# First batch of attention: where the probabilities are normalised and where the threshold is made

## The chip, the cores and the metric

One core of a Trainium2 chip runs the whole program. The metric is the device time of one execution in microseconds (us), as a median of several runs. The five engines appear in the profile as PE (TensorE matmul), PEld (TensorE's weight load, which overlaps PE), DVE (VectorE), ACT (ScalarE), POOL (GpSimd) and SP (SyncE, which issues the DMAs here). Each engine works through its own instruction list strictly in order.

## The reference

Attention with a threshold, then two feed-forward layers. Everything is float32.

```python
# q, k, v: (4, 8, 576, 64), tau = 0.02
scores = scale * q @ k.T                       # per batch and head, 576 x 576
thresh = max(scores, axis=-1) - tau
scores = where(scores >= thresh, scores, -1e9)
attn = exp(scores - max(scores)) ; attn = attn / (sum(attn) + 1e-9)
x = (attn @ v)  -> (2304, 512)
g = x @ w_gate ; x = (g * sigmoid(g) * (x @ w_val)) @ w_out      # 512 -> 1536 -> 512
h = max(x @ w_in, 0) ; out = (h * h) @ w_out2                    # 512 -> 2048 -> 512
```

## The kernel before

**Tiles.** Attention goes through 144 tiles of 128 query rows: 4 batches, 4 pairs of heads in each, 9 tiles in a pair. The first batch is tiles 0 to 35. The loop over `i` in `attention_moe` issues, for each turn, the steps of several tiles at different stages (`lag` is 2). The steps of one tile t are:

- QK: the scores on TensorE into one of two PSUM tiles `s` (t modulo 2).
- RED: the negated row maximum `nm` on VectorE (line 587).
- EXP: `e = exp(s + nm)` on ScalarE into one of three SBUF tiles `e` (t modulo 3), line 593, and right behind it the threshold `thr = -nm - tau`, a single column of 128 values, on ScalarE (line 595).
- MASK: one VectorE instruction multiplies `e` by `s >= thr` and sums each row (line 604). It is the last reader of `s`, so QK of tile t + 2 waits for it.
- RCP: the reciprocal `r` of the sum, one column, on VectorE (line 610).
- NORM: `e = e * r` over 128 x 576 values on GpSimd (line 615).
- TR: TensorE transposes the five 128-wide blocks of `e` into PSUM banks (line 635). It frees `e` for EXP of tile t + 3.
- PH, PL: copies of the transposed blocks from PSUM to SBUF, mostly on ScalarE in the first batch (the name `x` in the profile, line 48), a few on VectorE (line 50).
- AV: probabilities times values on TensorE (line 691 in the first batch, 694 later).

**Work beside it.** Throughout the first batch and the first half of the second one a loader turns the float64 weights into pairs of float32 pieces: each piece is a DMA (line 121), one ScalarE instruction (line 130), four VectorE instructions on 128 x 256 values (lines 132, 134, 138, 140), a ScalarE copy `w` (line 48) and a GpSimd subtraction `w` (line 56). For every coming pair of heads the queries and keys are split (`land` on ScalarE, `raw` on VectorE line 527 and on GpSimd line 56) and moved by DMA, a small block `qt` and the values `vs` are made on GpSimd (lines 52, 56). Once a batch's attention is done, its first feed-forward matmuls (line 219, input `xs_m`) fill TensorE between the tiles of the next batches. After attention TensorE runs the rest of the two layers.

**Order.** The instruction lists are fixed when the program is built. A scheduler sorts by the order of issue, shifted by offsets that the tables `early0` (first batch) and `early` (later) give each step; a step with a positive offset moves ahead of what was issued before it.

Of the kernel before, what the change touches and what calls it, by code (L numbers as in the profile page):

```python
# [14 lines left out]
ALU = mybir.AluOpType  # L15
# [4 lines left out]
B, H, S, D = 4, 8, 576, 64  # L20
# [42 lines left out]
def attention_moe(tc, qkv, qk0, tau, w1, w2, out, cfg):  # L63
    nc = tc.nc
# [8 lines left out]
    tau_n = cpool.tile([P, 1], F32, name="tau_n")  # L73
# [337 lines left out]
    for i in range(2):  # L411
        t = [ptp.tile([P, P], F32R, name=f"qt{i}{j}", tag=f"qt{i}{j}") for j in range(2)]
# [146 lines left out]
    st = [dict() for _ in range(NTILE + 8)]  # L559
# [30 lines left out]
    def EXP(t):  # L590
        e = es[t % len(es)]
        st[t]["e"] = e
        nc.scalar.activation(e[:, :S], st[t]["s"][:, :S], AF.Exp, bias=st[t]["nm"])  # L593
        if cfg["thr"] == "A":
            nc.scalar.activation(st[t]["thr"], st[t]["nm"], AF.Identity, scale=-1.0, bias=tau_n)  # L595
        else:
            e = nc.vector if cfg["thr"] == "D" else nc.gpsimd
            e.tensor_scalar(st[t]["thr"], st[t]["nm"], scalar1=-1.0, scalar2=tau_n, op0=ALU.mult, op1=ALU.add)

    def MASK(t):  # L600
        e = st[t]["e"]
# [10 lines left out]
    def NORM(t):  # L612
        e = st[t]["e"][:, :S]
        r = st[t]["r"]
        nc.gpsimd.tensor_scalar(e, e, scalar1=r, scalar2=1.0, op0=ALU.mult, op1=ALU.mult)  # L615

# [188 lines left out]
    for i in range(NTILE + lag + 1):  # L807
        mp1.age += 1
        fstate["i"] = i
        t = i - lag - 1  # L810
# [10 lines left out]
        if i < NTILE:  # L821
            at_(RED, i)
            at_(EXP, i)
# [7 lines left out]
        if 0 <= i - 1 < NTILE:  # L831
            at_(RCP, i - 1)
            at_(NORM, i - 1)
# [123 lines left out]
def pack(inputs):  # L957
# [15 lines left out]
    def cols(w, nf):  # L973
# [32 lines left out]
    "u1": ("P", "P"),  # L1006
    "u2": ("A", "D"),
    "qs": "A",
    "thr": "A",
    "wl": "PD",  # L1010
    "live": (3, 2),
    "fill": 6,
    "om": "A",
    "early0": {
        "AV": -2, "PS": 16, "NORM": 34, "EXP": 32, "LA": 20, "FP": -100, "PL": 30, "fill_group": -40,
        "RED": -12, "RCP": 4, "MASK": 4, "NEG": -60,
    },
    "three": 20,
# [29 lines left out]
```

## Time and profile before

| | us |
|---|---|
| median of 3 runs (1197.79 to 1198.41) | 1198.29 |
| the profiled execution | 1198.72 |
| span of its trace | 1196.9 |
| VectorE busy in the first batch, 11 to 113 us | 85.84 of 102.00 |
| TensorE busy in the same stretch | 94.18 of 102.00 |
| TensorE busy from 200 us on | 988.64 of 996.00 |

The span is what the trace covers; 1.8 us of the execution's own time lie around it. Busy times of TensorE are an upper reading, since its matmuls overlap and their ends are modelled. In the tables below, "idle before" is time in which an engine stood still ahead of an instruction, with the instruction that released it.

### The profile page before, as it was taken

To read this page: it belongs to the slowest core of one execution; us is meant where nothing else is said; L and a number is where in the kernel's file an instruction comes from. 1 tells how busy PE (TensorE), PEld (TensorE's weight loads), DVE (VectorE), ACT (ScalarE), POOL (GpSimd) and SP (SyncE) were. 2 spreads that over 40 slices of the span, in tenths; PEclk is the share of its full clock that TensorE was granted. 3 is DMA by queue.
4 is the path that set the end of the run, shared out by engine and by line. 5 is a ranking of instruction groups with operands and counts; after the bars stand their busy time and mean duration, and the time that the engine had idled before them with its cause. 6 is when DMAs were issued, how large, how long until landed. Compare 5 with 4: busy or idle time off the path is not lost.

```text
span 1196.9 us, 20191 instructions
## 1 busy us (share of the span) xinstructions
PE 1162.6 (97%) x7008; PEld 1074.8 (90%) x7008; DVE 868.2 (73%) x2143; ACT 652.1 (54%) x1622; POOL 293.8 (25%) x417
## 2 busy tenths in 40 slices
PE   5999998999999999999999999999999999999998
PEld 4555887999999999999999999999999899999997
DVE  6877997799989895789965954468449748754443
ACT  5777887888777774545432532145546425533221
POOL 4445875676776663000000000000000000000000
PEclk9999998999999999999999999999999999999999
DMA  5664452444334310332310300003002201100111
GB/s 177 151 182 127 127 134 66 109 116 110 94 97 106 93 36 1 108 104 80 98 36 7 108 29 1 1 18 104 21 1 80 62 1 54 36 1 1 53 54 53
DMA packets 40853, 84.79 MB, mean 71 GB/s; under 512 B 5936, under 2 KB 6960, under 8 KB 40752
## 3 DMA queue, kind: packets, MB, share of 16 engines
q1 hardware_dynamic: 40752, 83.52, 24.9%
q8 instruction: 55, 0.90, 0.3%
q14 instruction: 46, 0.38, 0.1%
HBM read 52.23 MB, written 4.72 MB: 48 GB/s over the span
## 4 chain that ended last, share of the span: by engine, by line
PE 79%; DVE 9%; DMA 3%; ACT 3%; issue 2%; POOL 2%; SPq 1%; POOLq 0%; DVEq 0%; ACTq 0%
PE mm L219 30%; PE mm L310 15%; PE mm L264 9%; PE s L575 5%; PE bank L635 5%; PE bank L219 4%; PE bank L264 4%; PE bank L694 4%; PE bank L691 3%; DMA wr<-in_w_dram 2%; DVE e L604 2%; DVE nm L587 1%; POOL e L615 1%; DMA raw<-in_qkv_dram 1%; DVE xs_k L56 1%
## 5 line engine op out<-in xcount | busy, mean ns | idle before, releaser
L219 PE MATMUL mm<-xs_k,w 128*128 128x384 f32 (+1 forms) x2400 | 413.2, 330 | 0.5 <-ACT x L48 0.5
L219 PEld LDWEIGHTS mm<-xs_k,w 128*128 128x128 f32 x2400 | 407.8, 188 | 2.5 <-ACT x L48 0.7
L310 PE MATMUL mm<-w,k_u 128*128 128x512 f32 x864 | 201.3, 391 | 0.3 <-DVE k_u L56 0.3
L310 PEld LDWEIGHTS mm<-w,k_u 128*128 128x128 f32 x864 | 161.5, 188 | 34.0 <-DVE k_u L56 1.0
L635 PE MATMUL bank<-ident,e 128*128 128x128 f32 x720 | 162.9, 278 | 6.4 <-POOL e L615 1.9
L219 PE MATMUL bank<-xs_m,w 128*128 128x288 f32 x720 | 137.1, 325 | 2.4 <-DVE xs_m L56 1.7
L615 POOL TENSOR_SCALAR e<-e,r 128x576 f32<-128x576 f32 x144 | 113.8, 791 | 83.6 <-DVE r L610 34.4
L604 DVE SCALAR_TENSOR_TENSOR e<-s,thr,e 128x577 f32<-128x577 f32 x144 | 117.0, 813 | 14.7 <-ACT thr L595 7.2
L48 ACT ACTIVATE k_u<-k_th 128x384 fp32r<-128x384 f32 (+1 forms) x148 | 76.3, 516 | 90.0 <-DVE k_th L294 47.0
L587 DVE TENSOR_REDUCE nm<-s 128x1 f32<-128x576 f32 x144 | 108.3, 753 | 17.7 <-PE s L575 16.6
L635 PEld LDWEIGHTS bank<-ident,e 128*128 128x128 f32 x720 | 95.2, 141 | 28.7 <-issue 15.9
L56 DVE TENSOR_TENSOR k_u<-k_th,k_u 128x384 fp32r<-128x384 f32 (+1 forms) x148 | 81.2, 549 | 47.8 <-ACT k_u L48 47.4
L219 PEld LDWEIGHTS bank<-xs_m,w 128*128 128x128 f32 x720 | 111.1, 189 | 5.1 <-DVE xs_m L56 3.4
L593 ACT ACTIVATE e<-s,nm 128x576 f32<-128x576 f32 x144 | 107.4, 746 | 14.3 <-PE bank L635 7.0
L655 ACT ACTIVATE pt<-bank 128x384 fp32r<-128x384 f32 (+1 forms) x216 | 92.1, 437 | 35.1 <-PE bank L635 28.9
L293 ACT ACTIVATE k_th<-mm 128x384 f32<-128x384 f32 x96 | 46.3, 483 | 111.0 <-PE mm L219 110.9
L264 PE MATMUL mm<-k_u,w 128*128 128x384 f32 (+1 forms) x624 | 106.1, 327 | 0.6 <-DVE k_u L56 0.4
L264 PEld LDWEIGHTS mm<-k_u,w 128*128 128x128 f32 x624 | 103.7, 188 | 1.0 <-DVE k_u L56 0.6
L694 PE MATMUL bank<-pt,vs 128*128 128x256 f32 (+1 forms) x480 | 93.5, 324 | 1.3 <-POOL pt L56 1.2
L575 PE MATMUL s<-kh,qs 128*128 128x288 f32 x256 | 78.1, 319 | 14.2 <-DVE qs L484 7.2
L294 DVE TENSOR_TENSOR k_th<-k_th 128x384 f32<-128x384 f32 x96 | 53.3, 555 | 52.4 <-ACT k_th L293 52.1
L48 ACT ACTIVATE w<-wf 128x256 fp32r<-128x256 f32 x116 | 46.8, 413 | 57.0 <-DVE wf L140 43.3
(90 smaller groups left out, 1697.0 us busy)
## 6 DMA issues: line engine op xcount, KB each, us to landing
wr<-in_w_dram SPq DMA_DIRECT2D x106, 256.0 KB, 3.0
raw<-in_qkv_dram SPq DMA_DIRECT2D x15, 896.0 KB, 4.7
kh<-land SPq DMA_DIRECT2D x60, 144.0 KB, 2.5
kl<-raw SPq DMA_DIRECT2D x60, 144.0 KB, 2.7
xF<-in_w_dram SPq DMA_DIRECT2D x30, 256.0 KB, 2.9
out_dram<-xF SPq DMA_DIRECT2D x18, 256.0 KB, 2.0
qs<-land SPq DMA_DIRECT2D x30, 144.0 KB, 2.4
qs<-raw SPq DMA_DIRECT2D x30, 144.0 KB, 2.6
```

The lines of the kernel that those rows point to most:

```text
L48: nc.scalar.activation(out, in_, AF.Copy)
L56: e.tensor_tensor(out, a, b, op=ALU.subtract)
L219: mm(pt[:, :n], w[:, a, col + c * P : col + (c + 1) * P], xs[:, b, c, :], start=(i == 0), stop=(i == len(TERMS) - 1),)
L264: mm(pt[:, :n], w[:, a, 2 * DM + m * P : 2 * DM + (m + 1) * P], u[:, b, :], start=(k == 0), stop=(k == last),)
L310: mm(pt, u[:, b, s * P : (s + 1) * P], w[:, a, DM : 2 * DM], start=(k == 0), stop=(k == last),)
L575: mm(sp[:, cols], l, r[:, cols], start=(n_ == 0), stop=(n_ == len(pairs) - 1),)
L587: nc.vector.tensor_reduce(nm, sv, axis=AX.X, op=ALU.max, negate=True)
L593: nc.scalar.activation(e[:, :S], st[t]["s"][:, :S], AF.Exp, bias=st[t]["nm"])
L604: nc.vector.scalar_tensor_tensor(e, st[t]["s"][:, : S + 1], st[t]["thr"], e, op0=ALU.is_ge, op1=ALU.mult, accum_out=sum_)
L615: nc.gpsimd.tensor_scalar(e, e, scalar1=r, scalar2=1.0, op0=ALU.mult, op1=ALU.mult)
L635: mm(dst[:, j], e[:, c0 : c0 + P], ident, is_transpose=True, start=(j == 0), stop=(j == len(cols) - 1),)
L694: mm(o[:, :n], hd["vs"][:, SLOT[k % 5], :], pt[:, k, lo : lo + n], start=(k == 0), stop=(k == 9))
```

## The change

In tiles 0 to 35 NORM goes from GpSimd to VectorE, with one multiplication in place of two, and the threshold goes from ScalarE to GpSimd. In the first batch's table the offset of NORM goes from 34 to 4, that of RCP. Later tiles keep both steps where they were.

```diff
@@ EXP
         nc.scalar.activation(e[:, :S], st[t]["s"][:, :S], AF.Exp, bias=st[t]["nm"])
-        if cfg["thr"] == "A":
+        if t >= cfg["normd"]:
             nc.scalar.activation(st[t]["thr"], st[t]["nm"], AF.Identity, scale=-1.0, bias=tau_n)
         else:
-            e = nc.vector if cfg["thr"] == "D" else nc.gpsimd
-            e.tensor_scalar(st[t]["thr"], st[t]["nm"], scalar1=-1.0, scalar2=tau_n, op0=ALU.mult, op1=ALU.add)
+            nc.gpsimd.tensor_scalar(st[t]["thr"], st[t]["nm"], scalar1=-1.0, scalar2=tau_n, op0=ALU.mult, op1=ALU.add)
@@ NORM
-        nc.gpsimd.tensor_scalar(e, e, scalar1=r, scalar2=1.0, op0=ALU.mult, op1=ALU.mult)
+        if t < cfg["normd"]:
+            nc.vector.tensor_scalar(e, e, scalar1=r, scalar2=None, op0=ALU.mult)
+        else:
+            nc.gpsimd.tensor_scalar(e, e, scalar1=r, scalar2=1.0, op0=ALU.mult, op1=ALU.mult)
@@ CFG
-    "thr": "A",
+    "normd": 36,
     "early0": {
-        "AV": -2, "PS": 16, "NORM": 34, "EXP": 32, "LA": 20, "FP": -100, "PL": 30, "fill_group": -40,
+        "AV": -2, "PS": 16, "NORM": 4, "EXP": 32, "LA": 20, "FP": -100, "PL": 30, "fill_group": -40,
```

The list of VectorE before, in the last pair of heads of the first batch, from MASK of tile 27 (sum_963) on: MASK, RCP and the loader's steps, and the reductions of tiles 29 and 30 (nm_999, nm_1030) between them.

```order
L604 SCALAR_TENSOR_TENSOR e_95,sum_963<-s_108,thr_932,e_95 128x577
L56 TENSOR_TENSOR xs_m_1340<-xF,xs_m_1340 128x288
L610 RECIPROCAL r_964<-sum_963 128x1
L604 SCALAR_TENSOR_TENSOR e_96,sum_994<-s_107,thr_970,e_96 128x577
L587 TENSOR_REDUCE nm_999<-s_108 128x1
L610 RECIPROCAL r_995<-sum_994 128x1
L587 TENSOR_REDUCE nm_1030<-s_107 128x1
```

The same place of VectorE's list now, where lines are numbered a little differently (603 is MASK, 609 RCP, 615 NORM):

```order
L603 SCALAR_TENSOR_TENSOR e_95,sum_963<-s_108,thr_932,e_95 128x577
L603 SCALAR_TENSOR_TENSOR e_96,sum_994<-s_107,thr_970,e_96 128x577
L609 RECIPROCAL r_964<-sum_963 128x1
L140 SCALAR_TENSOR_TENSOR xF<-xF 128x256
L615 TENSOR_SCALAR e_95<-e_95,r_964 128x576
L609 RECIPROCAL r_995<-sum_994 128x1
L132 TENSOR_SCALAR xF<-xF 128x256
L615 TENSOR_SCALAR e_96<-e_96,r_995 128x576
L587 TENSOR_REDUCE nm_999<-s_108 128x1
L134 TENSOR_SCALAR xF<-xF 128x256
L587 TENSOR_REDUCE nm_1030<-s_107 128x1
L138 SCALAR_TENSOR_TENSOR xF<-xF 128x256
```

Two tiles now go side by side: two MASKs, then the two NORMs among the loader's steps, then two reductions. The xs_m subtraction has left this place.

GpSimd's list before, at the preparation of the fifth pair of heads, with NORM of tiles 30 (r_1059) and 31 (r_1087):

```order
L615 TENSOR_SCALAR e_95<-e_95,r_1059 128x576
L52 TENSOR_SCALAR vs_1205<-raw_1020 128x5x64
L52 TENSOR_SCALAR vs_1275<-raw_1020 128x5x64
L56 TENSOR_TENSOR vs_1205<-raw_1020,vs_1205 128x5x64
L56 TENSOR_TENSOR vs_1275<-raw_1020,vs_1275 128x5x64
L56 TENSOR_TENSOR raw_1020<-raw_1020,land_1022 128x288 x2
L56 TENSOR_TENSOR w_2_145<-wf_78,w_2_145 128x256
L615 TENSOR_SCALAR e_96<-e_96,r_1087 128x576
```

The same place of GpSimd's list now (line 597 is the threshold; thr_1031 is that of tile 30, thr_1064 that of tile 31):

```order
L597 TENSOR_SCALAR thr_1031<-nm_1030,tau_n 128x1
L52 TENSOR_SCALAR vs_1275<-raw_1020 128x5x64
L56 TENSOR_TENSOR vs_1205<-raw_1020,vs_1205 128x5x64
L56 TENSOR_TENSOR vs_1275<-raw_1020,vs_1275 128x5x64
L56 TENSOR_TENSOR raw_1020<-raw_1020,land_1022 128x288 x2
L56 TENSOR_TENSOR w_2_145<-xF,w_2_145 128x256
L597 TENSOR_SCALAR thr_1064<-nm_1063,tau_n 128x1
```

The threshold of tile 31 stands where NORM of the same tile stood, behind the values, the keys and one weight piece.

At the end of the first batch VectorE's list now has the four xs_m subtractions of the first fill block almost together, behind the reduction of tile 38 (nm_1322):

```order
L587 TENSOR_REDUCE nm_1322<-s_108 128x1
L609 RECIPROCAL r_1316<-sum_1315 128x1
L56 TENSOR_TENSOR xs_m_1340<-xF,xs_m_1340 128x288 x3
L140 SCALAR_TENSOR_TENSOR wf_78<-xF,wf_78 128x256
L56 TENSOR_TENSOR xs_m_1340<-xF,xs_m_1340 128x288
```

Before, two of the four stood ahead of the first batch's end. From about tile 50 on the lists of VectorE and TensorE hold the same steps at the same tiles as before.

## Rows read from the trace of the kernel before

**Rows 1.** Busy time by stretch: stretch, length, then each engine's busy time (instructions).

```profile
core 0: us, PE busy (x) PEld busy (x) DVE busy (x) ACT busy (x) POOL busy (x), PEclk, DMA share, GB/s
11.00:113.00 102.00, 94.18 (x481) 58.40 (x482) 85.84 (x215) 76.70 (x196) 49.56 (x71) 1.00 0.55 145
113.00:140.00 27.00, 26.16 (x182) 22.98 (x181) 22.72 (x57) 22.07 (x62) 18.83 (x26) 1.00 0.45 128
140.00:170.00 30.00, 26.74 (x191) 24.53 (x190) 28.99 (x69) 25.18 (x68) 23.04 (x31) 1.00 0.49 132
170.00:200.00 30.00, 24.66 (x147) 21.73 (x147) 27.40 (x67) 22.98 (x60) 17.33 (x23) 0.89 0.34 95
200.00:1196.00 996.00, 988.64 (x6007) 945.17 (x6005) 699.77 (x1729) 501.81 (x1234) 179.60 (x252) 1.00 0.20 57
```

**Rows 2.** Waits, 11 to 113 us: who waited for whom, total, times, longest.

```profile
PEld s L575 <- DVE e L604: 8.4, 5, 4.4
...
DVE nm L587 <- PE s L575: 7.9, 14, 1.2
...
DVE e L604 <- ACT thr L595: 4.6, 5, 1.3
...
PEld bank L635 <- POOL e L615: 4.1, 7, 1.2
```

**Rows 3.** ScalarE's exponential and threshold, 11 to 113 us: groups, busy us, mean ns.

```profile
L593 ACT ACTIVATE e<-s,nm 128x576 f32<-128x576 f32 x38 | 28.2, 742 | 11.0 <-PE bank L635 7.0 <-DVE nm L587 1.4 <-POOL w L56 0.9
...
L595 ACT ACTIVATE thr<-nm,tau_n 128x1 f32<-128x1 f32 x37 | 10.6, 291 | 0.2 <-DVE nm L587 0.2
```

**Rows 4.** GpSimd's NORM and its smallest multiplication, 11 to 113 us, groups.

```profile
L615 POOL TENSOR_SCALAR e<-e,r 128x576 f32<-128x576 f32 x37 | 29.0, 787 | 35.2 <-DVE r L610 14.4 <-PE bank L635 4.7 <-ACT xF L48 4.2
...
L52 POOL TENSOR_SCALAR qt<-qs 128x64 fp32r<-128x64 f32 x9 | 2.5, 274 | 2.8 <-DMA qs<-raw 2.8
```

**Rows 5.** VectorE, 500 to 1190 us, where GpSimd is idle: groups by shape.

```profile
L56 DVE TENSOR_TENSOR k_u<-k_th,k_u 128x384 fp32r<-128x384 f32 x138 | 76.7, 556 | 47.6 <-ACT k_u L48 47.2
...
L138 DVE SCALAR_TENSOR_TENSOR wf<-wr,wf 128x256 int32<-128x256 int32 x100 | 41.8, 420 | 0.7
L56 DVE TENSOR_TENSOR w<-wf,w 128x256 fp32r<-128x256 f32 x101 | 41.7, 421 | 6.4 <-ACT w L48 5.9
...
L134 DVE TENSOR_SCALAR wf<-wf 128x256 int32<-128x256 int32 x100 | 28.6, 288 | 0.6
```

**Rows 6.** VectorE one after another: start, length, line; first near 27, then near 89 us.

```profile
27.21 0.29 DVE L132 TENSOR_SCALAR xF<-xF 128x256 f32<-128x256 f32 x1
27.42 0.16 DVE L610 RECIPROCAL r<-sum 128x1 f32<-128x1 f32 x1
...
89.00 0.76 DVE L587 TENSOR_REDUCE nm<-s 128x1 f32<-128x576 f32 x1 [0.94 <-PE s L575]
89.68 0.15 DVE L610 RECIPROCAL r<-sum 128x1 f32<-128x1 f32 x1
```

**Rows 7.** Busy time of VectorE's lines 132, 134, 138, 140, in that order.

```profile
11.00:113.00 102.00, 4.65 (x13) 1.00 0.55 145
...
11.00:113.00 102.00, 6.70 (x14) 1.00 0.55 145
...
11.00:113.00 102.00, 6.42 (x14) 1.00 0.55 145
...
11.00:113.00 102.00, 6.78 (x14) 1.00 0.55 145
```

**Rows 8.** VectorE's xs_m subtraction in the first batch, group of 11 to 113 us.

```profile
L56 DVE TENSOR_TENSOR xs_m<-xF,xs_m 128x288 fp32r<-128x288 f32 x3 | 1.7, 566 | 0.0
```

**Rows 9.** GpSimd in order of time near 98 us.

```profile
98.52 1.60 POOL L56 TENSOR_TENSOR raw<-raw,land 128x288 fp32r<-128x288 f32 x2
100.08 0.78 POOL L56 TENSOR_TENSOR w<-wf,w 128x256 fp32r<-128x256 f32 x1
100.84 0.74 POOL L615 TENSOR_SCALAR e<-e,r 128x576 f32<-128x576 f32 x1
```

## The prediction, made before the changed kernel ran

> **What bounds the kernel now.** I read the stretches first [rows 1]. From 200 us on TensorE is busy for 988.64 of 996 us, at full clock: nothing can be won there, and whatever the part before 200 us gains or loses arrives at the end unchanged. The change touches tiles 0 to 35, that is 11 to 113 us. In that stretch no engine is full: TensorE 94.18 of 102 us, VectorE 85.84, ScalarE 76.70, GpSimd 49.56. Next come the waits of that stretch [rows 2], which say why it still takes 102 us: TensorE and VectorE hold each other up. TensorE's QK stands 8.4 us for a MASK that has not freed its scores, its transposes 4.1 us for NORM; VectorE stands 7.9 us for scores and 4.6 us in MASK for the threshold, five times, up to 1.3 us. So the first batch is paced by a loop through four engines, and the engine with the least air after TensorE is VectorE, with 16.2 us. That is the engine that gets the work. Right behind, from 140 to 170 us, VectorE is busy 28.99 of 30 us: it can be run to 0.966, and it has no air to take over what the first batch leaves undone.
>
> **The change, part by part.**
>
> *The threshold leaves ScalarE.* 36 instructions of 0.291 us [rows 3]. ScalarE is not full, so the 10.5 us are worth only what waits for them: MASK need no longer wait for EXP and then for thr, but for the later of the two. Of the 4.6 us that MASK waited for thr the part behind EXP was about 5 x 0.29 = 1.5 us; the rest was EXP itself.
>
> *The threshold on GpSimd.* No row shows a one-column operation there. From above it is bounded by the 128 x 64 multiplication, 0.274 us [rows 4], from below by nothing; I take 0.2 us, nearer to the row, 36 x 0.2 = 7.2 us on an engine that gives up more. It starts with EXP from the same `nm` and has 0.742 us until EXP ends [rows 3], so it is hidden unless GpSimd is still at something else. If that cover goes, MASK waits, and behind MASK on VectorE's list stand RCP, NORM and the reductions, for which TensorE waits.
>
> *NORM leaves GpSimd.* 36 instructions of 0.787 us [rows 4]. TensorE's 4.1 us of waiting for it go. So does a queue: once, NORM starts only after 1.60 us of keys and 0.78 us of a weight piece [rows 9].
>
> *NORM on VectorE.* This is the price on which all hangs, and the trace of before has no VectorE multiplication of this size. The nearest rows: with GpSimd idle, the one-input, SBUF-to-SBUF step of line 134 takes 288 ns for 256 values, the two-input steps of the same width 420 and 421 ns, and 556 ns for 384 [rows 5]. Two-input work costs (556 - 421) / 128 = 1.055 ns a value; one-input work, at the same fixed part, half of that (421 - 0.5 x 1.055 x 256 = 286, the row says 288). NORM has one tensor input and a column of scalars. At the half rate it takes 288 + 320 x 0.527 = 457 ns, at the full rate 421 + 320 x 1.055 = 759 ns. Followed by the next instruction at once, it takes 0.08 us less of the engine's time: a 0.29 us step starts 0.21 us ahead of the next, a 0.76 us reduction 0.68 us ahead [rows 6]. So 36 x 0.38 = 13.7 us, or 36 x 0.68 = 24.5 us. I take 13.7: the operation is of line 134's kind, float32 in SBUF with one tensor input, and only the scalar's kind differs.
>
> The Trainium skill, "VectorE: DVE Perf Modes" (the perf-mode tier table), states the same split, 1227 ns against 2293 ns for 2048 float32 values, for tensor_scalar against tensor_tensor. An estimate from that page would be 0.46 us for NORM, which the trace's 0.457 us agrees with; the sum stays as it is.
>
> *What VectorE and GpSimd cost each other.* Lines 132 and 134 take 4.65 + 6.70 = 11.35 us for 27 instructions in the first batch [rows 7], against 27 x 0.288 = 7.8 alone [rows 5]: 3.6 us, 0.13 each, lost while GpSimd is busy 0.49 of the time. Lines 138 and 140 lose 6.42 + 6.78 - 28 x 0.420 = 1.4 us. NORM is 29.0 of GpSimd's 49.56 us [rows 1, 4]; with it gone 0.58 x 5.0 = 2.9 us of this loss go. GpSimd keeps 20.6 us and gets 7.2, 0.27 of the stretch, so a NORM on VectorE loses 0.13 x 0.27 / 0.49 = 0.07 us, 36 of them 2.6 us. Net: -0.3 us.
>
> A harder case: the Trainium skill, "SBUF — State Buffer" (SBUF: two separate sides), says that the port pair that VectorE's double-rate and two-input instructions share with GpSimd is an exclusive lock, held for a whole instruction while the other blocks. By it, a NORM that meets a GpSimd step of 0.78 us waits 0.39 us on average, in 0.27 of the cases, 3.8 us in all instead of 2.6: an estimate from that rule of 1197.1 us. Line 134's 0.13 us says less than the rule, which would make it 0.49 x 0.39 = 0.19.
>
> *What the scheduler moves along.* Two xs_m subtractions of 0.566 us [rows 8], 0.49 in a row, leave the first batch for the start of the second: -1.0 us here. There VectorE is busy 22.72 of 27 us [rows 1], so of the 1.0 us I count 0.4 as coming back.
>
> **The sum.** What VectorE has to do in the first batch: 85.84, minus 19 x 0.08 = 1.5 for the ends that show only because the two largest kinds of wait follow [rows 2, 6], plus 13.7, minus 0.3, minus 1.0, makes 96.7 us. With no wait at all the stretch would be 96.7 us, at the 0.966 of the second batch 100.1 us. I take 0.975, because two tiles now stand side by side in VectorE's list and each reduction has the partner's work ahead of it: 99.2 us, 2.8 less than 102. With the 0.4 us that come back, 2.4 us. TensorE allows it, at 94.18 us. The profiled execution took 1198.72 us (span 1196.9 and 1.8 around it), 0.4 above the median; the sum there is 1196.3, on the median's footing 1198.3 - 2.4 = **1195.9 us**. A difference under 0.2% (2.4 us) is about what a measurement of this kernel can't tell from none, and the forecast lies on that edge.
>
> **Rivals.**
>
> *VectorE becomes the bound (slower).* Place: VectorE's list in tiles 0 to 35. The stretch stays at 102 us only while VectorE's work stays under 102 x 0.975 = 99.5 us, that is while one NORM, port waits included, takes less than 0.45 + (99.5 - 96.7) / 36 = 0.53 us of the engine. At the full rate the work is 96.7 + 10.8 = 107.5 us, the stretch 110.3 us, the time 1207. At the half rate but with VectorE kept only 0.913 busy, as from 170 to 200 us (27.40 of 30) [rows 1], it is 105.9 us, and 1202.6. For it: 0.84 is all that VectorE reached in this stretch so far, and any loop through four engines loses something. Against it: two of that loop's links, thr behind EXP and NORM behind GpSimd's queue, are cut.
>
> *Hidden anyway (no change).* VectorE's air and TensorE's 4.1 us cancel, or the gain is given back from 113 to 200 us, where VectorE is at 0.97 and 0.91 and TensorE stands 3.3 and 5.3 us of 30 twice [rows 1], partly for the coming pairs' data, which a faster first batch does not bring. The same comes of a NORM that always sits out a whole GpSimd step (3.8 us of port waits, 1197.1). Time 1197 to 1200. For it: the lists hold the same steps from tile 50 on.
>
> *The threshold is stuck (slower).* In the new list thr of tile 31 stands behind the values, the keys and a weight piece. That is 1.60 + 0.78 = 2.4 us [rows 9] after the keys' input is there; VectorE has NORM, a reduction and loader steps to do meanwhile, some 2.5 us. If half of the keys' 1.60 us shows at each of 4 pairs, 3.2 us are lost, and the gain of 2.4 turns into 0.8 us of loss: 1199; if each of the 13 weight pieces delays a MASK by half its length too, another 5 us, 1204. It decides against the change from 2.4 us of such waits on.
>
> **Chances.** Forecast (1192.5 to 1198) 0.50, of which 0.37 lie below 1195.9 and 0.13 above; VectorE as the bound 0.20, of which 0.01 inside 0.2%; hidden anyway 0.20, of which 0.03 below, 0.14 inside and 0.03 above; the threshold stuck 0.10, of which 0.02 inside. Faster by over 0.2%: 0.37 + 0.03 = 0.40; same 0.13 + 0.01 + 0.14 + 0.02 = 0.30; slower 0.19 + 0.03 + 0.08 = 0.30. The range that keeps 8 in 10 begins at 1189.5: with no wait at all on VectorE the time is 1193, and TensorE, at 94.18 us, leaves room for a few us more. It ends at 1206, which takes in the half-rate case of the first rival and the stuck threshold and stops just short of the full rate.
>
> **What the next profile would show.** Right, if NORM on VectorE means 0.46 to 0.55 us; if the stretch from the first to the 37th reduction is 98 to 101 us; if VectorE is at least 0.96 busy in it; if MASK's waits for thr and the transposes' waits for NORM are near nothing; if from tile 50 on everything stands about 2.5 us earlier. Wrong, if NORM is 0.75 us, if QK waits for MASK by clearly more than 8.4 us, if MASK waits for thr on GpSimd, or if the second batch takes longer by what the first won.

## The result, and the profile of the changed kernel

The changed kernel takes 1213.78 us (median of 4 runs, 1211.85 to 1216.0) beside 1198.35 us of the kernel before: 1.0125 times as long, 95% interval 1.0102 to 1.0148. The forecast was 1195.9 us, with a range up to 1206 and 0.30 for slower. The profiled execution took 1216.0 us, its span is 1214.2.

The stretches of the changed kernel, in the columns of [rows 1]:

```profile
11.00:113.00 102.00, 87.51 (x434) 55.64 (x435) 87.37 (x218) 62.92 (x141) 31.13 (x65) 0.96 0.48 129
113.00:140.00 27.00, 24.95 (x128) 15.90 (x127) 20.28 (x52) 17.42 (x44) 8.97 (x14) 0.94 0.41 112
140.00:170.00 30.00, 27.64 (x202) 25.91 (x200) 28.80 (x71) 24.52 (x66) 23.96 (x33) 1.00 0.48 131
170.00:200.00 30.00, 24.42 (x163) 21.28 (x164) 29.03 (x68) 24.26 (x66) 20.90 (x28) 1.00 0.51 137
200.00:1196.00 996.00, 987.22 (x6013) 944.82 (x6012) 710.88 (x1757) 512.05 (x1262) 188.46 (x262) 1.00 0.20 56
```

In the first 102 us TensorE gets through 434 matmuls where it had 481 [rows 1], ScalarE through 141 instructions (of its 196 some 37 were thresholds). GpSimd fell from 49.56 to 31.13 us, as it should. But VectorE, with 36 more instructions of half a microsecond each in the batch, is busy 87.37 us, hardly more than the 85.84 before: it did not fill up, it waits. From 200 us on TensorE is as full as before. Nearly the whole loss is made by the first batch and its end.

To see how much of it is waiting, take the preparation of the seventh pair of heads on VectorE (line 527, the sixth of its kind; the first pair is prepared elsewhere) as a mark. It starts at 155.53 us before and at 171.41 after. Busy time up to that mark, first before, then after:

```profile
11.00:155.50 144.50, 134.34 (x763) 94.61 (x764) 123.17 (x308) 112.06 (x291) 79.64 (x111) 1.00 0.52 142
```

```profile
11.00:171.40 160.40, 140.52 (x761) 97.66 (x762) 137.84 (x343) 105.70 (x254) 64.80 (x112) 0.97 0.47 128
```

The same TensorE work, 761 and 763 matmuls, takes 15.9 us longer: 9.7 us of that is TensorE standing still (19.9 against 10.2 us), 6.2 us a longer busy time, to which a mean granted clock of 0.97 against 1.00 adds. The spans of these two traces differ by 17.3 us (1214.2 against 1196.9), so nearly all of the loss is there.

The waits of 11 to 113 us after the change, as in [rows 2]:

```profile
ACT x L48 <- PE bank L637: 17.4, 21, 2.5
PEld s L575 <- DVE e L603: 12.3, 12, 4.3
ACT xF L48 <- PE bank L693: 11.4, 11, 2.6
...
DVE e L603 <- ACT e L593: 6.5, 10, 1.4
DVE nm L587 <- PE s L575: 5.2, 6, 1.8
PEld bank L693 <- ACT x L48: 4.6, 11, 1.0
PEld bank L637 <- ACT x L48: 4.0, 5, 2.1
```

QK waits for MASK 12 times, 12.3 us, where it was 5 times, 8.4 us [rows 2]. The transposes' waits for NORM are small (1.0 us on the weight loads, 4.1 before), and MASK has no wait for the threshold in that stretch at all. What grew most are the rows with ScalarE in them. Its waits before, for the transposes and for AV, which [rows 2] does not hold:

```profile
ACT x L48 <- PE bank L635: 10.0, 17, 1.6
...
ACT xF L48 <- PE bank L691: 1.7, 4, 0.5
```

From 10.0 + 1.7 us they went to 17.4 + 11.4. Behind ScalarE, MASK stands for EXP, and AV and the transposes for ScalarE's copies.

One place shows how these hang together. Instructions of the changed kernel in order of time (start, length, engine):

```profile
90.20 2.91 PE L693 MATMUL bank<-x 128*64 128x320 f32 x10
...
90.47 0.52 DVE L615 TENSOR_SCALAR e<-e,r 128x576 f32<-128x576 f32 x1
90.90 0.16 DVE L609 RECIPROCAL r<-sum 128x1 f32<-128x1 f32 x1
...
91.93 0.76 DVE L587 TENSOR_REDUCE nm<-s 128x1 f32<-128x576 f32 x1
...
93.15 0.49 ACT L48 ACTIVATE xF<-bank 64x64 f32<-64x64 f32 x2 [2.58 <-PE bank L693]
...
94.20 0.77 ACT L48 ACTIVATE x<-bank 128x384 f32<-128x384 f32 x2
...
95.33 0.49 ACT L48 ACTIVATE x<-bank 128x384 f32<-128x384 f32 x1 [0.36 <-PE bank L637]
95.72 0.73 ACT L593 ACTIVATE e<-s,nm 128x576 f32<-128x576 f32 x1
95.87 2.37 PE L693 MATMUL bank<-x 128*64 128x256 f32 x10 [0.36 <-ACT x L48]
...
96.55 0.82 DVE L603 SCALAR_TENSOR_TENSOR e<-s,thr,e 128x577 f32<-128x577 f32 x1 [1.39 <-ACT e L593]
...
98.17 0.40 PE L575 MATMUL s<-kh,qs 128*128 128x288 f32 x1
```

TensorE does an AV as one block from 90.20 on. ScalarE has the copies of its output next in its list and stands 2.58 us for them (before, the longest such wait is 0.5 us). The row maximum that EXP needs is there at 92.69, but EXP stands behind those copies, a weight piece and the copies of two tiles, and starts at 95.72, 3.0 us late. MASK on VectorE waits 1.39 us for it, and the next QK comes at 98.17, behind the next whole AV. No engine is busy beyond its means here; each does, in order, what its list says next.

The added and moved instructions themselves (count; shortest, median and longest in ns; first and last start):

```profile
L615 DVE TENSOR_SCALAR e<-e,r x36: 500/515/1060, 14.6 to 128.3; 128x576 f32<-128x576 f32 x36
```

```profile
L597 POOL TENSOR_SCALAR thr<-nm,tau_n x36: 262/268/643, 12.0 to 121.7; 128x1 f32<-128x1 f32 x36
```

### The profile page after: what moved, and what is told of

It is laid out like the page before. It is cut to its first block, busy times and chain, and to the rows that moved or that the text cites. A ratio compares the mean times of both kernels' runs of the same rounds, so it can differ in the third digit from the quotient of the medians.

```text
span 1214.2 us, 20139 instructions
## 1 busy us (share of the span) xinstructions
PE 1168.4 (96%) x7008; PEld 1077.5 (89%) x7008; DVE 884.5 (73%) x2179; ACT 646.6 (53%) x1586; POOL 278.4 (23%) x417
## 4 chain that ended last, share of the span: by engine, by line
PE 80%; DVE 10%; ACT 3%; DMA 3%; issue 2%; POOL 1%; SPq 0%; POOLq 0%; DVEq 0%; ACTq 0%
PE mm L219 32%; PE mm L310 16%; PE mm L264 8%; PE s L575 5%; PE bank L637 5%; PE bank L219 4%; PE bank L264 4%; PE bank L693 3%; PE bank L696 3%; DVE e L603 2%; DVE nm L587 2%; DMA xF<-in_w_dram 1%; DMA wr<-in_w_dram 1%; DVE xs_m L56 1%; DVE pt L56 1%
## 5 line engine op out<-in xcount | busy, mean ns | idle before, releaser
L603 DVE SCALAR_TENSOR_TENSOR e<-s,thr,e 128x577 f32<-128x577 f32 x144 | 116.9, 814 | 17.4 <-ACT e L593 11.6
L617 POOL TENSOR_SCALAR e<-e,r 128x576 f32<-128x576 f32 x108 | 86.0, 796 | 56.3 <-DVE r L609 28.6
L323 DVE TENSOR_TENSOR xF<-xF,mm 128x512 f32<-128x512 f32 x54 | 37.0, 686 | 55.8 <-PE mm L310 55.8
```

The source lines that it names most:

```text
L603: nc.vector.scalar_tensor_tensor(e, st[t]["s"][:, : S + 1], st[t]["thr"], e, op0=ALU.is_ge, op1=ALU.mult, accum_out=sum_)
```

## The experiments

Times in the table are medians, the ratio is to the kernel before in runs on the same chip, with its 95% interval. Kernels have their own line numbers; where a row is shown, the text says what it is.

| run | NORM / threshold on | lists | us | ratio |
|---|---|---|---|---|
| norm_only | VectorE / ScalarE | scheduler | 1216.7 | 1.0147 (1.0132 to 1.0162) |
| thr_only | GpSimd / GpSimd | scheduler | 1205.7 | 1.0053 (1.0038 to 1.0068) |
| norm_pinned | VectorE / ScalarE | of before | 1201.8 | 1.0021 (1.0011 to 1.0030) |
| thr_pinned | GpSimd / GpSimd | of before | 1201.5 | 1.0019 (1.0003 to 1.0035) |
| both_pinned | VectorE / GpSimd | of before | 1203.2 | 1.0041 (1.0026 to 1.0056) |
| lists_of_after | GpSimd / ScalarE | of after | 1215.9 | 1.0140 (1.0125 to 1.0155) |
| col1_lists_before | VectorE, 1 column / GpSimd | of before | 1196.2 | 0.9980 (0.9965 to 0.9995) |
| col1_lists_after | VectorE, 1 column / GpSimd | of after | 1211.8 | 1.0104 (1.0081 to 1.0126) |
| after_pe | VectorE / GpSimd | TensorE's of before | 1219.3 | 1.0175 (1.0158 to 1.0191) |
| after_act | VectorE / GpSimd | ScalarE's of before | 1218.8 | 1.0166 (1.0147 to 1.0186) |
| after_dve | VectorE / GpSimd | VectorE's of before | 1219.0 | 1.0173 (1.0150 to 1.0196) |
| free_dve | VectorE / GpSimd | of before, but VectorE's | 1215.8 | 1.0139 (1.0117 to 1.0161) |
| before_pairs | GpSimd / ScalarE | scheduler, one rule | 1200.3 | 1.0010 (0.9999 to 1.0021) |
| control_av | GpSimd / ScalarE | scheduler, other offset | 1201.0 | 1.0016 (1.0004 to 1.0029) |
| after_alt | VectorE / GpSimd | scheduler, one rule | 1209.0 | 1.0086 (1.0070 to 1.0101) |
| before_alt | GpSimd / ScalarE | scheduler, one rule | 1217.6 | 1.0155 (1.0135 to 1.0176) |
| norm_later | VectorE / GpSimd | scheduler, other offset | 1214.0 | 1.0127 (1.0109 to 1.0145) |
| after_tr3 | VectorE / GpSimd | scheduler, one rule | 1223.7 | 1.0206 (1.0187 to 1.0226) |

**Each move alone.** The offset of NORM (34 or 4) does not change a single row of any list, with either engine, so it needed no run. The two moves:

```diff
+        nc.scalar.activation(st[t]["thr"], st[t]["nm"], AF.Identity, scale=-1.0, bias=tau_n)   # norm_only
-        if t < cfg["normd"]:
-            nc.vector.tensor_scalar(e, e, scalar1=r, scalar2=None, op0=ALU.mult)                # thr_only
+        nc.gpsimd.tensor_scalar(e, e, scalar1=r, scalar2=1.0, op0=ALU.mult, op1=ALU.mult)
```

> NORM of tiles 0 to 35 on VectorE, the threshold stays on ScalarE; the lists come out new, as in the changed kernel. Theory of the lists (the fixed order of TensorE, ScalarE and VectorE that came out with the change stalls the first batch, not the added work): 1203 to 1216 us, by how bad these lists are. Theory of the work (36 NORMs at about 0.5 us are simply added to the loop over tiles): 1211 to 1216 us. Theory of the threshold (GpSimd makes it too late): about 1198 us.

> The threshold of tiles 0 to 35 on GpSimd, NORM stays on GpSimd. Theory of the lists: 1197 to 1206 us, these lists stand nearer to those of before. Theory of the work: 1195 to 1199 us, ScalarE loses 10 us and VectorE gains none. Theory of the threshold: about 1214 us.

NORM alone makes the whole loss, so the threshold is not needed for it. The threshold alone loses too, 6.4 us (beside 1199.3), but nothing comes on top when both move. These two runs leave open whether NORM's time or the new lists cost it.

**The lists held.** Edges that fix only the order of issue, between neighbours on one engine, make a kernel keep a list that another one had:

```diff
+    for earlier, later in zip(order, order[1:]):      # one list for each engine
+        tc.add_manual_dep(later, earlier.name,
+            mybir.DependencyInfo(mybir.DependencyClass.NoSync, mybir.DependencyReason.DATA), reason="order")
```

> NORM of tiles 0 to 35 on VectorE, directly behind RCP, and otherwise every engine keeps the list of the kernel before, instruction by instruction. Theory of the lists: 1196 to 1201 us, since VectorE's gaps in the first batch take up the added work. Theory of the work: 1210 to 1216 us, as in the changed kernel. Theory of the threshold: about 1198 us.

> The engines of the kernel before (NORM on GpSimd, threshold on ScalarE behind the exponential), but TensorE, ScalarE, VectorE and SyncE keep the lists of the changed kernel. Theory of the lists: 1209 to 1216 us, the loss comes with the lists though no work was moved. Theory of the work: 1196 to 1200 us. Theory of the threshold: about 1198 us.

> The whole change (NORM on VectorE behind RCP, threshold on GpSimd), but every engine keeps the list of the kernel before for all the rest; only the place of the threshold in GpSimd's list is the scheduler's. If the lists are the whole loss: 1197 to 1203 us, near the run with NORM alone in the lists of before (1201.8). If threshold and NORM together cost something that neither does alone: 1208 us or more.

> The threshold of tiles 0 to 35 on GpSimd, and every engine keeps the list of the kernel before for all the rest. If a threshold on GpSimd beside the exponential is hidden: 1195 to 1200 us. If it is late behind GpSimd's other work, or slowed beside VectorE, and MASK waits for it: 1202 to 1208 us.

This decides between lists and work. The whole change in the lists of before loses 4.6 us; the work of before in the lists of the changed kernel loses 16.5 us (beside 1199.3 on the same chip), with not one instruction moved to another engine. The profile of that second kernel, 11 to 113 us (line numbers of before), has the waits of the changed kernel, not those of its own engines:

```profile
ACT x L48 <- PE bank L635: 16.6, 21, 2.3
DVE e L604 <- ACT thr L595: 14.8, 20, 1.6
...
ACT xF L48 <- PE bank L691: 10.4, 10, 2.5
...
PEld bank L691 <- ACT x L48: 5.1, 12, 1.2
PEld bank L635 <- ACT x L48: 4.0, 4, 2.4
```

And both_pinned, with VectorE's added work in the lists of before, hasn't (line numbers of the changed kernel):

```profile
PEld s L575 <- DVE e L603: 14.7, 14, 4.4
...
ACT x L48 <- PE bank L637: 6.6, 13, 1.8
PEld bank L637 <- ACT x L48: 3.3, 5, 1.0
...
ACT xF L48 <- PE bank L693: 2.2, 4, 0.7
DVE e L603 <- ACT e L593: 1.4, 2, 0.8
```

```profile
11.00:113.00 102.00, 91.41 (x459) 56.49 (x460) 95.34 (x241) 68.49 (x152) 37.52 (x69) 1.00 0.52 138
```

ScalarE is no longer stuck, VectorE is busy 0.935 of the stretch, and what QK waits for is MASK behind VectorE's own work. norm_pinned and both_pinned end 0.8 and 0.2 us above the ranges given for the lists, and far below the 1208 and 1210 us of their rivals. thr_pinned came out between its two expectations: a threshold on GpSimd is not a gain even in the old lists.

**NORM's time alone.** The two runs below keep every row of all five lists and cut only the width of NORM:

```diff
-            nc.vector.tensor_scalar(e, e, scalar1=r, scalar2=None, op0=ALU.mult)
+            nc.vector.tensor_scalar(e[:, :1], e[:, :1], scalar1=r, scalar2=None, op0=ALU.mult)
```

> The changed kernel with all lists kept as they are, but NORM of tiles 0 to 35 works on one column of 576 (so the first batch is hardly normalised). VectorE loses 36 times some 0.45 us, 16 us. If the lists by themselves stall the first batch: 1206 us or more, most of the loss stays. If the changed lists only put NORM's 0.5 us on the path, tile after tile: 1194 to 1200 us. Between the two, the loss divides.

> The changed kernel in the lists of before (1203.2 us with whole NORMs), NORM of tiles 0 to 35 on one column of 576 (so the first batch is hardly normalised). If the 4.6 us lost in these lists are NORM's time on VectorE: 1195 to 1199 us. If they come from the threshold on GpSimd or from elsewhere: 1201 to 1204 us.

With both_pinned and the changed kernel they make a square. In the lists of before NORM's time is worth 1203.2 - 1196.2 = 7.0 us; in the lists of after 1213.8 - 1211.8 = 2.0 us, no more than the runs of either scatter. The lists are worth 10.6 us with whole NORMs and 15.6 us without. A NORM of one column takes 0.21 us, a whole one in the mean 0.56 us in the lists of before and 0.59 in those of after, so the cut takes 12.5 and 13.8 us of VectorE's work away, less than the 16 expected. In col1_lists_after ScalarE sits out the same wait for the same AV, though NORM takes 0.2 us:

```profile
91.88 0.75 DVE L587 TENSOR_REDUCE nm<-s 128x1 f32<-128x576 f32 x1
93.70 0.49 ACT L48 ACTIVATE xF<-bank 64x64 f32<-64x64 f32 x2 [2.58 <-PE bank L693]
...
96.28 0.74 ACT L593 ACTIVATE e<-s,nm 128x576 f32<-128x576 f32 x1
```

**What in the lists.** First one engine's list at a time, with the edges above:

> The changed kernel with TensorE's list of before; the other lists come out of the scheduler under that. If the order of TensorE (probabilities times values in whole blocks ahead of the scores) is the loss: 1198 to 1204 us. If it is ScalarE's or VectorE's order, whose lists here stand about as far from before as from the changed kernel: 1208 to 1216 us.

> The changed kernel with ScalarE's list of before (less the thresholds); the other lists come out of the scheduler under that, TensorE's then much like that of before, VectorE's not. If ScalarE's or TensorE's order is the loss: 1198 to 1204 us. If VectorE's order is: 1208 to 1216 us.

> The changed kernel with VectorE's list of before (NORM directly behind RCP); the other lists come out of the scheduler under that and stand as far from before as the changed kernel's do. If VectorE's order (two MASKs, two NORMs and two reductions together) is the loss: 1198 to 1204 us. If TensorE's or ScalarE's order is: 1208 to 1216 us.

None of the three brings anything back; each is 5 us slower than the changed kernel and above both ranges of its expectation. Holding one list is thus no cure. It clears no engine's order either, since the lists that were left free moved again. Then rules and offsets:

```diff
+    chain_(tc, [x_ for k in range(36) for x_ in (reds[k + 1], masks[k])])                        # after_alt, before_alt
+    chain_(tc, [x_ for k in range(1, 36, 2) for x_ in (reds[k], reds[k + 1], masks[k], masks[k + 1])])  # before_pairs
+    for k in range(2, 35): chain_(tc, [qks[k + 3], trs[k][0]])                                    # after_tr3
-        "AV": -2, "PS": 16, "NORM": 34,
+        "AV": -6, "PS": 16, "NORM": 34,                                                           # control_av
-        "AV": -2, "PS": 16, "NORM": 4,
+        "AV": -2, "PS": 16, "NORM": -30,                                                          # norm_later
```

> The changed kernel with one rule more for VectorE's list of the first batch: reductions and MASKs alternate (RED of tile t + 1, MASK of tile t, RED of t + 2, MASK of t + 1), where the changed kernel has two reductions and then two MASKs; all else is the scheduler's. Theory of the pairs (the two score tiles are freed together, so TensorE and VectorE wait for each other): 1198 to 1206 us. Theory of the kept balance (the lists of before fit the durations on the chip by their tuned offsets, and any other set of lists loses, whatever its kind): 1208 to 1220 us.

> The kernel before (NORM on GpSimd, threshold on ScalarE) with one rule more for VectorE's list of the first batch: two reductions, then the two MASKs, as in the changed kernel; all else is the scheduler's. Theory of the pairs: 1208 to 1216 us. Theory of the kept balance: 1203 to 1212 us, some loss as with any other lists.

> The kernel before with the offset of AV in the first batch's table at -6 in place of -2: no work is added, removed or moved to another engine, but a quarter of TensorE's and a fifth of VectorE's rows of the first batch come in another order. Theory of the pairs: 1196 to 1202 us, since reductions and MASKs still mostly alternate. Theory of the kept balance: 1203 to 1212 us.

Two theories of mine fell here. Pairs of reductions and MASKs cost the kernel before nothing that can be told (1.0010). Nor does just any rearrangement cost much: the control lost 0.16%. What helped the changed kernel a little, alternation, is not good in itself, as before_alt shows below.

> The changed kernel with one number other: the offset of NORM in the first batch's table is -30 in place of 4, so that the scheduler puts NORM, and with it the transposes and their copies, later. In TensorE's list the transposes of tile t stand behind the scores of tile t + 3 for 31 of 32 tiles (19 of 32 in the changed kernel, 30 of 32 before). Theory of the distance (short distance makes TensorE and ScalarE, in order, wait for tile t's own chain before they go on with t + 2 and t + 3): 1199 to 1206 us. Rival (lists that the scheduler makes with NORM on VectorE are bad in VectorE's own order, between loader and loop): 1210 to 1220 us.

> The changed kernel with one rule for TensorE's list: the transposes of tile t stand behind the scores of tile t + 3 (all 32 tiles, 19 of 32 without the rule); ScalarE's copies come later by that for some tiles only. Theory of the distance: 1201 to 1209 us, not all of it, since the copies still stand behind the exponential of t + 1 for 10 of 32 tiles. Rival: 1210 to 1220 us.

> The kernel before (NORM on GpSimd, threshold on ScalarE) with the rule of the earlier run that VectorE's reductions and MASKs alternate in the first batch; by it the transposes of all 32 tiles stand behind the scores of t + 2 only. Theory of the distance: 1205 to 1212 us, like the changed kernel with the same rule (1209.0). Rival: 1197 to 1203 us, as in the other runs with NORM on GpSimd.

> The changed kernel with the lists of before on TensorE, ScalarE, GpSimd and SyncE; VectorE's list alone is the scheduler's. Distances as before. Theory of the distance: 1201 to 1206 us, near the run with all lists of before (1203.2). Rival (VectorE's own order): 1210 to 1220 us.

The theory of the distance fell as well: norm_later has the long distance and stays at 1214, after_tr3 has it and is the slowest of all. free_dve is the clearest of the four: four engines have the lists of before, and VectorE's, made by the scheduler, still loses 12.6 us against both_pinned. So a new order on VectorE alone is enough to lose the time. It is not the only way: after_dve, with VectorE's list of before, takes 1219.0 us, and before_alt loses with no work moved. norm_later and free_dve came out in the range of their rival, VectorE's own order, after_tr3 and before_alt above both of theirs. Up to 113 us free_dve has a wait that the kernel before does not have, ScalarE standing for weight pieces that come later in VectorE's list than ScalarE's list reckons with:

```profile
ACT w L48 <- DVE xF L140: 11.1, 4, 3.8
...
ACT w L48 <- DVE wf L140: 3.1, 1, 3.1
```

So the lists of before work as a set. One pattern goes through all the slow runs, those of 1209 us and more: what stands behind ScalarE waits in order. Up to 113 us either AV's weight loads wait 4.4 us or more for ScalarE's copies, or MASK waits 10.1 us or more for EXP (after_act, free_dve, after_pe, after_tr3). In the kernel before and in all runs up to 1206 us the first is 2.3 us at most and the second 9.3. That is read off the traces, the limits were picked with the times in hand, and 9.3 and 10.1 lie close together; no run changed either wait alone, so it is not shown as the cause.

## Why the prediction was wrong, by its own steps

**The step that failed** is "I take 0.975, because two tiles now stand side by side in VectorE's list and each reduction has the partner's work ahead of it". VectorE was busy 87.37 of 102 us, 0.857, and 0.850 from the first reduction to the 37th. The new lists were in front of me, and I read them on VectorE alone, as a gain. In their place the runs showed a loss: by the square above the lists cost 10.6 to 15.6 us. What I did not follow is ScalarE, where an EXP now stands behind copies that wait for a whole AV. That the loss comes by this way is read off the traces and not shown by a run: with ScalarE's list of before (after_act) it is 20 us.

The stretch from the first to the 37th reduction, forecast at 98 to 101 us, was 109.8. Before, after, and in both_pinned:

```profile
L587 DVE TENSOR_REDUCE nm<-s x37: 734/758/759, 10.9 to 109.1; 128x1 f32<-128x576 f32 x37
```

```profile
L587 DVE TENSOR_REDUCE nm<-s x37: 732/746/758, 11.1 to 120.9; 128x1 f32<-128x576 f32 x37
```

```profile
L587 DVE TENSOR_REDUCE nm<-s x37: 742/751/759, 11.2 to 113.6; 128x1 f32<-128x576 f32 x37
```

The first line shows a slip in the prediction's own sign besides: from the first to the 37th reduction the kernel before took 98.2 us, not 102. A gain of 2.8 us would have meant some 95.4 there, and "98 to 101" would have passed for right with no gain at all.

**NORM's price was nearly right.** Forecast 0.457 us alone, measured 0.515 in the median: the half rate, far from 0.759. One after another they start 0.43 us ahead of the next instruction, where the sum had 0.38. The waits for GpSimd were forecast at 2.6 us and came to 2.6: the mean is 0.588, 36 x (0.588 - 0.515). They fell on seven NORMs, five of them twice as long as the rest.

**The threshold's price was too low, the wait rightly small.** 0.268 us instead of 0.2, just under the upper bound of 0.274. MASK did not wait for it in this profile, so the third rival is out as the cause. But that leaving ScalarE was worth something is not borne out: thr_pinned is 1.0019.

**The sum would have been wrong without the lists too.** In the lists of before the change gives 1203.2 us. VectorE is at 0.935 there, and the first rival's case of half rate at 0.913 busy gave 1202.6. That rival came nearest to what the work costs, though the close number is partly luck: with 0.935 in place of 0.913 its own sum gives 96.7 / 0.935 = 103.4 us, and 1200.1. Nearly nothing spoke for 0.975 where [rows 1] had 0.913 and 0.966 as the nearest stretches. And the most that could be had was known badly: without NORM's time the gain is 2.2 us (0.9980), about the 2.4 that I forecast with it.

**What was right:** that what the part before 200 us loses arrives at the end nearly unchanged (15.9 us at the mark, 17.3 at the end); that waits between four engines, and no full engine, set the length of the stretch; and the sign to look for, QK waiting for MASK by clearly more than 8.4 us (12.3).

**What stays open:** which neighbours in the lists make the most of the loss, whether it runs through ScalarE's waits, and why the scheduler arranges them so once NORM is on VectorE. Three simple accounts of it were tried: pairs and distance fell, and no single engine's list accounts for all the runs.

## What to carry to other kernels

When a change goes through a scheduler, cost its lists and its work apart: pin the old lists and run the new work, pin the new lists and run the old work. Read new lists on every in-order engine, above all on the one that serves several stages, and ask at each row that the next stage needs what stands in front of it and what that waits for. Idle time on an engine in a loop of four is not room for work: here 16 us of gaps took in 36 half-microsecond steps at a cost of some 7 us, measured against steps of 0.21 us, with the order of everything else in place.

## What the runs showed of the hardware that was not expected

How long a NORM on VectorE takes is settled by what GpSimd does when it starts. Instructions of the changed kernel near 29, 57 and 112 us:

```profile
29.20 0.51 DVE L615 TENSOR_SCALAR e<-e,r 128x576 f32<-128x576 f32 x1
29.45 0.39 POOL L597 TENSOR_SCALAR thr<-nm,tau_n 128x1 f32<-128x1 f32 x1 [2.28 <-DVE nm L587]
...
57.03 0.74 POOL L56 TENSOR_TENSOR w<-xF,w 128x256 fp32r<-128x256 f32 x1 [1.51 <-ACT w L48]
57.47 0.61 DVE L615 TENSOR_SCALAR e<-e,r 128x576 f32<-128x576 f32 x1
...
112.44 0.75 POOL L56 TENSOR_TENSOR w<-wf,w 128x256 fp32r<-128x256 f32 x1 [2.16 <-ACT w L48]
112.51 0.99 DVE L615 TENSOR_SCALAR e<-e,r 128x576 f32<-128x576 f32 x1
```

A NORM that starts inside a two-input GpSimd step ends 0.31 to 0.32 us behind that step's end: 57.47 + 0.61 against 57.03 + 0.74, and 112.51 + 0.99 against 112.44 + 0.75. Seven did, and took 0.59 to 1.06 us; the other 29 took 0.50 to 0.53. The other way round, a threshold that starts inside a NORM ends behind it, and takes 0.38 us or more in place of 0.26. Neither engine shares; the later one waits. The Trainium skill, "SBUF — State Buffer" (SBUF: two separate sides), says just that of the port pair of these two engines, and the traces agree: my own sum, with a rate of loss, had the amount right (2.6 us) and the manner wrong. A NORM of one column does not wait: all 36 of col1_lists_after take 0.19 to 0.21 us, the seven that start inside a two-input GpSimd step too.

TensorE's granted clock followed the stalls. Within four microseconds in which it was busy for 1.73 the clock fell, to 0.65 in the mean, and the next four ran at 0.50, which is 1.2 GHz:

```profile
108.00:112.00 4.00, 1.73 (x8) 1.49 (x9) 4.00 (x12) 2.52 (x6) 0.84 (x3) 0.65 0.60 129
112.00:116.00 4.00, 3.85 (x14) 2.34 (x13) 3.70 (x8) 1.80 (x4) 1.28 (x3) 0.50 0.22 66
```

In both_pinned the clock stays at 1.00 over the whole first batch. But the low clock is not what the loss needs: norm_later takes 1214.0 us with the clock at 1.00 from 11 to 113 us, and on to 170:

```profile
11.00:113.00 102.00, 84.05 (x419) 54.04 (x420) 82.44 (x209) 61.30 (x137) 34.03 (x64) 1.00 0.48 129
```
